# Block 0 goes into the FFN unscaled, and its inverse RMS is applied to the gate in PSUM and to the output rows

## The chip, the cores and the metric

The kernel runs on one core of one Trainium2 chip. A time is the device time of one execution in microseconds (us). Before the change the median of 9 runs is 244.38 us (243.91 to 245.1).

## What is computed

Two stages follow each other. The first is attention with four sink tokens and a causal window of 128, for 4 sequences of 768 tokens and 8 heads of 64. The second takes the heads side by side as x (3072 tokens of 512) through a normalisation and a gated FFN:

```
keep   = is_sink | in_window
a      = softmax(where(keep, q @ k.T / 8, -1e9));  attn = a @ v
x      = attn, heads side by side                       # 3072 x 512
xn     = x / sqrt(mean(x*x) + 1e-6) * rms_g
g, val = xn @ w_gate, xn @ w_val                        # 512 x 1536 each
out    = (g * sigmoid(g) * val) @ w_out                 # 1536 x 512
```

## The kernel before

The 3072 tokens are 24 blocks of 128 (six to a sequence), and four blocks are a group G of 512 columns for the FFN. Group 0 is worked on while its blocks are still being made: the list HAND cuts its FFN into 12 pieces f.0 to f.11, of which f.0, f.1, f.2, f.4, f.6 and f.7 take the first 256 columns (blocks 0 and 1), and f.0 is cut once more into block 0 and block 1 (`split`). Later groups are worked through whole, with the attention of coming blocks put between the parts.

A block g goes through these atoms, each named by a token of the string ORDER ("v.2.0/1" is atom 1 of v for block 2, half 0): t or T transpose q and k on TensorE (lines 281, 298); b puts the additive masks into PSUM by a matmul (382); s or S are the scores and their exp on ScalarE (394, 442); sk, sv, ss and a are the sinks (324 to 380, 489); v is the product with v, with reciprocal and normalisation on VectorE (504); q squares x with an accumulated sum (538); y makes the inverse RMS by six tiny VectorE instructions (557); xr scales the rows by it (610); x transposes the scaled rows and copies them to xnt, for blocks 0 and 1 with rms_g as a column gt (634, 647). Then mms (662) multiplies xnt by the weights: gate into `pg`, value into `pvl`, tanh on ScalarE, and `first` and `second` on VectorE make hT = (tanh(pg/2) + 1) * pg * pvl (lines 680 to 701). out_atoms (750) multiplies by w_out, and line 764 moves the result out of PSUM times 0.5. gt and gb (251, 263) bring rms_g to columns and to a full tile by float32 matmuls of one row.

Order is by hand: until group 1 the scheduler is off for all five engines, and each engine takes its instructions in the order in which the tokens of ORDER (849) issue them. w.N is a filler: a matmul of zeros, 512 columns wide, that nobody reads (242). ON_ACT and ON_DVE (220) say which of ScalarE and VectorE does a movable copy or square. PSUM has 8 banks of 512 float32 columns from one pool, and a tile waits until the bank's last reader is done. Loads are issued by GpSimd (POOL) in the order of the string at line 200: q, k, v of a block, g and u the six chunks of w_gate and w_val, o the halves of w_out. LOADS and the loops of group and run (887, 839) place what comes later.

## Time and profile before

| what | value |
|---|---|
| median of 9 runs | 244.38 us |
| the profiled execution, own time | 244.68 us |
| its span | 242.8 us |
| TensorE (PE) busy | 237.7 us (98%) |
| VectorE (DVE) busy | 164.0 us (68%) |
| ScalarE (ACT) busy | 133.7 us (55%) |
| GpSimd (POOL) busy | 107.3 us (44%) |
| first FFN matmul starts (line 668) | 15.26 us |
| granted TensorE clock, mean of the span | 0.993 |

The profile is one execution, and times are counted from the start of its span. Part 1 of its page gives the busy time of each engine, part 2 the span in 40 slices of 6.1 us: a digit is a busy share in tenths, and PEclk is the granted TensorE clock in tenths of full speed. A row of a timeline reads: start, duration (of several merged instructions from the first start to the last end), engine, line of the kernel, operation, output and input, shape, count, and in brackets the idle time before it with what ended it. A busy TensorE can still be slow: the duration of a matmul includes its way through the pipe, and at half clock it just lasts longer. The pitch, from one start to the next, is what TensorE really spends.

### The profile page before, as it was taken

What the parts mean: (1) busy time and instruction counts of PE and PEld (TensorE: products, weight loads), DVE (VectorE), ACT (ScalarE), POOL (GpSimd) and SP (SyncE); (2) the same over time, 40 slices, a digit from 0 to 9 for tenths busy, and PEclk for the clock granted to TensorE, in tenths of its full rate; (3) what the DMA queues carried; (4) which work ended last, traced back from release to release, by engine and by line L of the source; (5) the groups of instructions that cost most, each with busy time, mean ns of one, the idle gap of its engine ahead of it and who ended that gap; (6) DMA issues with size and microseconds to landing.
All of it is one profiled execution on the core that took longest, in us unless ns stands there. A gap on an engine that the chain in (4) does not pass through costs nothing.

```text
span 242.8 us, 5281 instructions
## 1 busy us (share of the span) xinstructions
PE 237.7 (98%) x2011; PEld 137.5 (57%) x2011; DVE 164.0 (68%) x390; ACT 133.7 (55%) x309; POOL 107.3 (44%) x145
## 2 busy tenths in 40 slices
PE   8999999999999999999999999999999999999995
PEld 3668888855877874444444444444444444444443
DVE  5767796894988798067879086869077884287800
ACT  3675648458788874666562567664565342333212
POOL 8977686589649870389992003034032000000000
PEclk9979999999999999999999999999999999999999
DMA  9999999999999995489999664002600003600022
GB/s 128 143 178 186 182 166 199 176 155 175 208 152 122 62 110 67 89 223 155 139 145 96 173 159 84 0 1 38 189 35 3 0 0 70 173 19 1 0 79 97
DMA packets 109291, 26.56 MB, mean 109 GB/s; under 512 B 98385, under 2 KB 106321, under 8 KB 109266
## 3 DMA queue, kind: packets, MB, share of 16 engines
q0 software_dynamic: 80704, 13.90, 77.2%
q1 hardware_dynamic: 27378, 12.00, 23.9%
q10 hardware_dynamic: 1184, 0.33, 0.6%
q8 instruction: 16, 0.26, 0.5%
q14 instruction: 9, 0.07, 0.1%
HBM read 28.31 MB, written 6.29 MB: 143 GB/s over the span
## 4 chain that ended last, share of the span: by engine, by line
PE 95%; DVE 1%; DMA 1%; SPq 1%; ACT 0%; issue 0%; ACTq 0%
PE pg L668 26%; PE pvl L668 26%; PE po L757 22%; PE pT L455 4%; PE pv L516 3%; PE pv L520 3%; PE pqk L237 2%; PE pT L386 2%; PE pw L245 1%; PE po L739 1%; DMA qkT<-qs 1%; SPq L629 1%; PE pxt L642 1%; PE pv L497 1%; PE pT L401 1%; PE pss L367 1%
## 5 line engine op out<-in xcount | busy, mean ns | idle before, releaser
L668 PE MATMUL pvl<-xnt,wv 128*128 128x512 bf16 (+2 forms) x440 | 74.6, 306 | 0.0
L668 PE MATMUL pg<-xnt,wg 128*128 128x512 bf16 (+2 forms) x440 | 73.8, 305 | 0.5 <-DVE xnt L654 0.3
L687 DVE SCALAR_TENSOR_TENSOR p<-th,pg 128x512 bf16<-128x512 bf16 x72 | 49.3, 684 | 26.1 <-ACT th L682 25.6
L682 ACT ACTIVATE th<-pg 128x512 bf16<-128x512 f32 x72 | 43.2, 602 | 38.3 <-PE pg L668 38.1
L757 PE MATMUL po<-wo,hT 128*128 128x512 bf16 x276 | 62.3, 379 | 0.0
L697 DVE TENSOR_TENSOR hT<-p,pvl 128x512 bf16<-128x512 bf16 x72 | 49.2, 686 | 6.2 <-PE pg L668 0.5
L668 PEld LDWEIGHTS <-wv 128*128 128x128 bf16 x440 | 38.3, 98 | 24.8 <-issue 0.2
L668 PEld LDWEIGHTS <-wg 128*128 128x128 bf16 x440 | 37.5, 98 | 23.3 <-issue 1.3
L431 POOL TENSOR_SCALAR_AFFINE_SELECT et<-et 128x512 bf16<-128x512 bf16 x30 | 20.6, 692 | 65.4 <-ACT et L465 62.2
L757 PEld LDWEIGHTS <-hT 128*128 128x128 bf16 x276 | 26.3, 98 | 29.5
L465 ACT ACTIVATE et<-pT 128x512 bf16<-128x512 f32 x72 | 38.1, 606 | 5.7 <-PE pT L455 5.5
L764 ACT ACTIVATE osb<-po 128x512 f32<-128x512 f32 x23 | 13.7, 596 | 34.1 <-PE po L757 34.1
L551 ACT ACTIVATE sq<-x 128x256 bf16<-128x256 bf16 x42 | 17.6, 423 | 13.5 <-DVE x L532 13.3
L121 POOL DMA_DIRECT2D v<-in_v_dram x24 | 21.7, 903 | 7.6 <-DMA wo<-in_moe_w_out_dram 5.1
L527 DVE RECIPROCAL rden<-pv 128x4 f32<-128x4 f32 x48 | 7.6, 173 | 23.1 <-PE pv L520 23.1
L108 POOL DMA_DIRECT2D qs<-in_q_dram x23 | 20.8, 906 | 2.7 <-issue 0.8
L108 POOL DMA_DIRECT2D ks<-in_k_dram x23 | 20.7, 899 | 1.6 <-DMA wg<-in_moe_w_gate_dram 0.5
L532 DVE TENSOR_TENSOR x<-pv,rden 128x256 bf16<-128x256 f32 x48 | 19.4, 421 | 0.8
L622 DVE SCALAR_TENSOR_TENSOR xr<-x,y,gb 128x512 bf16<-128x512 bf16 x22 | 16.9, 816 | 0.2
L436 POOL TENSOR_SCALAR_AFFINE_SELECT et<-et 128x512 bf16<-128x512 bf16 x24 | 15.9, 660 | 0.0
L520 PE MATMUL pv<-v,et 128*128 128x65 bf16 x160 | 12.4, 194 | 0.0
L455 PE MATMUL pT<-qkT 64*128 64x256 bf16 (+1 forms) x160 | 11.3, 261 | 0.0
(82 smaller groups left out, 184.3 us busy)
## 6 DMA issues: line engine op xcount, KB each, us to landing
out_dram<-osb SPq DMA_DIRECT2D x21, 256.0 KB, 2.4
v<-in_v_dram POOLq DMA_DIRECT2D x24, 128.0 KB, 7.6
qs<-in_q_dram POOLq DMA_DIRECT2D x23, 128.0 KB, 7.1
ks<-in_k_dram POOLq DMA_DIRECT2D x23, 128.0 KB, 7.0
wv<-in_moe_w_val_dram POOLq DMA_DIRECT2D x6, 256.0 KB, 8.9
wg<-in_moe_w_gate_dram POOLq DMA_DIRECT2D x6, 256.0 KB, 8.6
wo<-in_moe_w_out_dram POOLq DMA_DIRECT2D x2, 768.0 KB, 11.1
out_dram<-osb SPq DMA_DIRECT2D x4, 128.0 KB, 3.1
```

Source lines behind the costliest of these rows:

```text
L108: nc.gpsimd.dma_start(out=tl, in_=src[b, :, t * P:(t + 1) * P, :].rearrange("h t d -> t h d"),)
L121: nc.gpsimd.dma_start(out=V16[b][:, t, :, 0:D], in_=v[b, :, t * P:(t + 1) * P, :].rearrange("h t d -> t h d"),)
L431: nc.gpsimd.affine_select(out=ev[:, :, 0, :], in_=ev[:, :, 0, :], compare_op=ALU.is_ge, fill=0.0, base=0, pattern=[[0, x], [1, P]], channe ...
L455: nc.tensor.matmul(out=banks[u][hi][:, j * w:(j + 1) * w], lhsT=QKT[b][pr, 1, hp, t * P:(t + 1) * P], rhs=QKT[b][pr, 0, hp, t * P:t * P + ...
L465: nc.scalar.activation(out=ets[u][:, hi].rearrange("p j n c -> p (j n c)"), in_=banks[u][hi], func=ACT.Exp, scale=inv_sqrt_d,)
L520: nc.tensor.matmul(out=dest, lhsT=E[(g, h, 0)], rhs=V16[b][:, t, h, :], start=(t == 0), stop=True, skip_group_check=True,)
L532: nc.vector.tensor_tensor(out=X16[g][:, heads_of(g, u), :], in0=view()[:, :, 0:D], in1=RDEN.pop((g, u)).unsqueeze(2).to_broadcast((P, 4, D ...
L668: nc.tensor.matmul(out=ps[:, i * w + c0:i * w + c0 + n], lhsT=w_sb[:, kt, ft * P:(ft + 1) * P], rhs=XNT[G][:, kt, cols], start=(kt == 0), ...
L682: LAST_TANH[0] = nc.scalar.activation(out=st["th"], in_=st["pg"], func=ACT.Tanh, scale=0.5).ins
L687: nc.vector.scalar_tensor_tensor(out=st["p1"], in0=st["th"], scalar=1.0, in1=st["pg"], op0=ALU.add, op1=ALU.mult,)
L697: LAST[0] = nc.vector.tensor_tensor(out=HT[key][:, i:i + n, cols], in0=st["p1"].rearrange("p (n c) -> p n c", n=n), in1=st["pvl"].rearrang ...
L757: nc.tensor.matmul(out=st["po"], lhsT=HT[(G, ft // 4)][:, ft % 4, tb * P:(tb + 1) * P], rhs=wo[:, ft, :], start=(ft == 0), stop=(ft == FTN ...
```

## The change

Block 0 is transposed as it comes from attention (X16), without xr. Its inverse RMS y is turned into a row that is equal in all partitions: a float32 matmul with y broadcast to 128 columns as the weights and a float32 identity as the moving operand, copied from PSUM to `yb`. In the six pieces of group 0 with blocks 0 and 1 in their columns, a new atom `scaled` multiplies block 0's 128 columns of each gate part in PSUM by yb, before the tanh. The value part stays unscaled; the missing factor comes in with block 0's output rows, which are moved out of PSUM times half0 = y / 2 in place of 0.5.

The string ORDER is another one as a whole, and ON_ACT, ON_DVE and the order of the loads are others too. It has 12 fillers in place of 9. gt and gb stand together, ahead of block 2's transposes.

```diff
+    half0 = const.tile([P, 1], FP32, name="half0")
-    raw = [opool.tile([P, DM], FP32, name="osb") for _ in range(3)]
+    raw = [opool.tile([P, DM], FP32, name="osb") for _ in range(4)]
+    ident32, yb = raw[3][:, 0:P], raw[3][:, P:2 * P]
...
+        nc.vector.tensor_copy(out=ident32, in_=ident)
...
-        for x in ("v0 q2 v1 k2 u0 g0 u2 v2 g1 g2 k3 u1 q3 g5 g3 u3 v3 g4 u4 v5 q4 u5 "
-                  "k4 q5 q6 k5 k6 o0 v4 o1 k7 q7 k8 v6 q9 v8 q8 v7 k9 v9").split():
+        for x in ("v0 v1 q2 u0 k2 v2 g0 g2 u2 g1 u1 k3 q3 g3 g4 u3 v3 g5 q4 u5 q5 u4 "
+                  "v5 k4 k6 v9 k5 k9 q6 v4 o0 o1 q7 k7 v7 v6 k8 v8 q9 q8").split():
...
+            if g0 == 0:
+                nc.vector.tensor_scalar(
+                    out=half0, in0=Y[0], scalar1=0.5, scalar2=None, op0=ALU.mult,
+                )
...
+    def a_yb():
+        ps = []
+
+        def mm():
+            ps.append(bank("pyb"))
+            nc.tensor.matmul(
+                out=ps[0][:, 0:P], lhsT=Y.pop(0).to_broadcast((P, P)), rhs=ident32,
+                start=True, stop=True,
+            )
+        return [mm, lambda: mover("yb", "a")(out=yb, in_=ps[0][:, 0:P])]
...
-            xr = XR.pop(g)
+            xr = XR.pop(g) if g else X16[g].rearrange("p h d -> p (h d)")
...
+        def scaled():
+            pg = st["pg"].rearrange("p (n c) -> p n c", n=n)[:, :, 0:P]
+            nc.vector.tensor_tensor(
+                out=pg, in0=pg, in1=yb.unsqueeze(1).to_broadcast((P, n, P)), op=ALU.mult)
+
         if split:
             return [lambda: half(0, 0), lambda: half(0, 1), lambda: half(1, 0), tanh,
-                    lambda: half(1, 1), first, second]
+                    lambda: half(1, 1), first, second, scaled]
+        if G == 0 and cols.start == 0:
+            return [gate, tanh, val, first, second, scaled]
...
-            nc.scalar.mul(osb, st["po"], 0.5)
+            nc.scalar.mul(osb, st["po"], half0 if G == 0 and tb == 0 else 0.5)
```

The part of ORDER from block 0's product with v to the second gate half of f.0, before:

```
        v.0.1/2 s.1.0/1 q.0.1/0 sk.0/0 s.1.0/2 s.0.1/2 v.0.0/2 q.0.0/0 y.0/0 gb/0 v.1.0/0
        v.1.0/1 b.2.0/0 sv.0/0 sv.0/1 y.0/1 y.0/2 v.1.0/2 y.0/3 y.0/4 w.74/0 gt/0 v.1.1/0
        t.2.0/0 y.0/5 xr.0/0 v.1.1/1 v.1.1/2 t.2.1/0 x.0/0 b.1.1/0 gt/1 q.1.0/0 t.2.0/1 s.1.1/0
        x.0/1 f.0/1 w.73/0 sv.0/2 q.1.1/0 y.1/0 y.1/1 y.1/2 y.1/3 y.1/4 y.1/5 sk.0/1 ss.0.2.1/0
        f.0/0 t.2.1/1 xr.1/0 x.1/0 s.2.0/0 gb/1 s.1.1/2 s.1.1/1 sv.0/3 ss.0.2.1/1 a.2/0 s.2.0/1
        s.2.0/2 x.1/1 f.0/2 f.0/3 v.2.0/0 v.2.0/1 v.2.1/0 f.0/4 f.1/0 v.2.0/2 v.2.1/1 q.2.0/0
```

and after:

```
        v.0.1/2 w.88/0 s.1.0/2 q.0.0/0 v.1.0/0 b.1.1/0 gt/0 gb/0 t.2.0/0 v.1.0/1 q.0.1/0 y.0/0
        y.0/1 y.0/2 v.1.0/2 s.0.1/2 x.0/0 y.0/3 gt/1 t.2.0/1 q.1.0/0 y.0/4 y.0/5 v.1.1/0 v.1.1/1
        v.1.1/2 yb/0 w.91/0 w.80/0 sv.0/0 t.2.1/0 s.1.1/0 x.0/1 q.1.1/0 y.1/0 y.1/1 y.1/2 sk.0/1
        y.1/3 y.1/4 yb/1 y.1/5 b.2.0/0 f.0/1 sv.0/2 ss.0.2.1/0 xr.1/0 f.0/0 x.1/0 sv.0/1 t.2.1/1
        s.2.0/0 f.0/7 s.1.1/1 s.1.1/2 ss.0.2.1/1 sv.0/3 s.2.0/1 w.90/0 s.2.0/2 x.1/1 a.2/0 f.0/2
        v.2.0/0 v.2.1/0 v.2.0/1 v.2.0/2 v.2.1/1 v.2.1/2 q.2.0/0 q.2.1/0 y.2/0 y.2/1 y.2/2 y.2/3
```

## The prediction, as it was put on record

> **What bounds the kernel now.** I read the engine table and the 40 slices first, then TensorE's timeline of the first 30 us beside VectorE's, then the busy times and granted clock in stretches, then the waits. Page, parts 1 and 2:

> ```profile
> PE 237.7 (98%) x2011; PEld 137.5 (57%) x2011; DVE 164.0 (68%) x390; ACT 133.7 (55%) x309; POOL 107.3 (44%) x145
> PEclk9979999999999999999999999999999999999999
> ```

> TensorE is busy 98% of the span. From about 27 us its matmuls follow each other at their own pitch, and the list of waits has only one later one that counts, 0.5 us for the transposes by DMA near 102 us, behind the same row of SyncE's queue in both kernels. So a change in block 0 pays only through what TensorE does before some 30 us. There the clock has a hole. Stretches of the first 22 us (width, then PE, PEld, DVE, ACT, POOL busy with instructions, PEclk, DMA share, GB/s):

> ```profile
> 5.20:8.61 3.41, 3.24 (x47) 1.89 (x46) 2.08 (x5) 1.40 (x4) 3.41 (x5) 1.00 2.17 139
> 8.61:12.02 3.41, 3.41 (x33) 2.11 (x33) 2.79 (x15) 2.69 (x8) 3.41 (x6) 1.00 1.57 142
> 12.02:15.44 3.42, 3.42 (x33) 2.39 (x33) 2.12 (x9) 2.41 (x9) 3.21 (x5) 0.50 1.50 165
> 15.44:18.85 3.41, 3.06 (x54) 2.46 (x53) 1.86 (x5) 2.73 (x7) 1.94 (x4) 1.00 1.66 190
> ```

> For 3.41 us TensorE ran at half speed, after a stretch in which it was "busy" throughout, but largely with float32 matmuls of one row (gb 1.05 us, gt 0.98 us, rows below). TensorE's timeline around it (start, us, engine, line, op):

> ```profile
> 8.87 1.12 PE L268 MATMUL pgb<-osb,gb 1*128 1x512 f32 x2
> ...
> 11.04 1.05 PE L257 MATMUL pgt<-gb,osb 1*128 1x1 f32 x8
> ...
> 13.29 0.63 PE L642 MATMUL pxt<-ident,xr 128*128 128x128 bf16 x4
> ...
> 15.26 0.69 PE L668 MATMUL pvl<-xnt,wv 128*128 128x128 bf16 x8
> ...
> 18.02 0.61 PE L668 MATMUL pg<-xnt,wg 128*128 128x128 bf16 x8 [0.33 <-DVE xnt L654]
> ```

> And VectorE's, for what these wait on:

> ```profile
> 11.84 0.39 DVE L618 TENSOR_SCALAR xr<-x,y 128x512 bf16<-128x512 bf16 x1
> ...
> 17.27 0.69 DVE L654 TENSOR_TENSOR xnt<-pxt,gt 128x512 bf16<-128x512 bf16 x1 [0.60 <-PE pxt L642]
> ...
> 24.67 0.68 DVE L687 SCALAR_TENSOR_TENSOR p<-th,pg 128x512 bf16<-128x512 bf16 x1
> 25.26 1.28 DVE L697 TENSOR_TENSOR hT<-p,pvl 128x512 bf16<-128x512 bf16 x2
> 26.82 0.69 DVE L687 SCALAR_TENSOR_TENSOR p<-th,pg 128x512 bf16<-128x512 bf16 x1 [0.28 <-ACT th L682]
> ```

> The reader should see that block 0's scaled rows are ready at 11.84 + 0.39 = 12.23 us, and TensorE comes to transpose them only at 13.29. The inverse RMS is not what TensorE waits for. Its real wait is block 1's copy (17.27 to 17.96), which holds the second half of the first gate until 18.02.

> **The change, part by part.** *Removed:* block 0's scaling (0.39 us of VectorE) and its place ahead of the transposes. On TensorE this is worth 0; with the clock full it would have come to the transposes some 0.5 us earlier, still after 12.2. Below zero nothing, above zero at most those few tenths.

> *Added on TensorE:* the broadcast matmul (float32, 128 columns) and fillers, 12 for 9, all three extra ones in mid-stream (five against two). The broadcast has no row. From below: one gt matmul of one column, 0.98 / 4 = 0.245 us. From above: gb with 512 columns, 1.05. By columns between them: 0.45. A filler of 512 columns is 0.22 us at full and 0.43 at half clock (the seven at the start begin 0.43 apart), so three are 0.65 to 1.3 us. Where TensorE waits anyway they are free.

> *Added on VectorE:* six scalings of 128x256 float32 in PSUM. No row reads and writes PSUM in place. Nearest is x<-pv,rden, 128x256 from PSUM, 0.42 us; a 512-wide copy of 0.68 bounds it above, 0.17 (the reciprocal's floor) below. I take 0.42, 2.5 us in all, four of them before 28 us. The copy of the broadcast row, half0 and the float32 identity are small (0.2, 0.1, 0.2 by the same floor). Against this, gb's copy (0.68) goes to ScalarE and xr of block 0 (0.39) goes. Each scaling stands between a gate and its tanh, so it also keeps a PSUM bank longer. The output's scale by half0 instead of 0.5 costs nothing: the same ACTIVATE of 0.60.

> *Moved:* v1, u0 ahead of k2, v2 ahead of the first gate weights. Loads land in the order of issue, 0.8 to 1.0 us per q, k or v and 1.2 to 2.1 per weight chunk, so by the bytes ahead of it g0 lands near 15.2 us (14.56 before) and u1 near 20.9 (21.6 before); both are in time in the walk below. Later, block 11's load changes places with block 14's in POOL's queue and now stands behind block 7's masks (63.2 to 65.8 us before). With 7.1 us to landing and 4.7 for its transposes by SyncE, which now pass one store, it is there near 77.5; block 10's scores, the first to read it, come at 81.6, so this costs nothing. gb and gt now stand together, ahead of block 2's transposes and block 1's second attention product.

> **The sum, by TensorE's queue.** I walk the new order with the pitches of the old timeline (start to start: 0.216 for 512 columns, 0.056 for 128, 0.03 for the 65-wide products; two rows of scores run side by side, so 16 matmuls take what 8 do) and hold each step until what it waits for is done. Both kernels are alike to 8.87 us. Then: filler to 9.09; block 1's product waits for the fourth exp (four end at 7.31 + 2.15 = 9.46) and takes to 9.75; masks 0.43, gt 0.98 to 11.2; gb 1.05. In the stretch 8.61 to 12.02 that is 0.2 + 0.2 + 0.25 + 0.43 us of bfloat16 work, 1.1, where the kernel before had some 1.25 and was slowed all the same. So I expect the half clock again from 12.02 to 15.44. Then gb ends at 12.5; eight transposes (0.107 each, as the four at 13.29) 13.35; the product's eight 13.8; broadcast about 0.65 14.45; two fillers 0.85 15.3; sink selection 15.5. From there at full clock t 0.22, scores 0.45, masks 0.43, first value half 0.45, sinks 0.28, first gate half 0.45: 17.78. VectorE then scales this half (17.9 to 18.3) *before* block 1's copy, which is queued behind it, 0.69: 19.0, against 18.02. The second gate half is queued behind that copy and all of TensorE behind it: **+1.0 us**. From there TensorE is full in both, and the lateness stays to the end. The profiled execution took 244.68 us (span 242.8); with 1.0 it is 245.7. The median of the nine runs is 0.3 below the profiled one, so I forecast **245.4**.

> [...]

> **Rivals.** *The fillers hold the clock (faster).* If it stays full from 12.02, the same queue gives gb to 12.25, transposes 12.7, product 12.95, broadcast 13.4, fillers 13.83, first value half 15.05, first gate half to 16.3; block 1's copy ends 17.65 and the second half starts at 17.7, 0.3 before. Before, block 2's products also stood still from 18.52 to 18.74 for an exp; here the exps are done first (18.05), and the value half behind the products ends at 19.1 and not at 19.75, 0.65 ahead. If that is kept: 244.38 - 0.65 = 243.7. For it: five fillers between 8.9 and 22 us. Against: less bfloat16 work ahead of 12.02 than before. It decides once PEclk is 1.00 there.

> *Full clock, but VectorE gives it back (level).* Between 22 and 28 us VectorE has 0.28 us idle before (third row above); three scalings come in. Each `first` or `second` takes 0.60 from start to start (24.67 to 25.26), and the matmuls of f.2 to f.4 wait for banks that these steps free. Walked on with that, the gate of f.4 starts at 27.55 (27.56 before) and that of f.8 at 36.9 (36.84): 244.4 to 244.7.

> *VectorE becomes the bound (slower still).* Half clock and the scalings at 0.68: four times 0.26 more on a queue without slack, 246.4.

> *It does not do what it says:* that the first FFN matmul, at 15.26 before, does not come earlier is my forecast itself (about 16.6).

> **How the numbers follow.** Forecast 0.52 (slower 0.50, same 0.02); clock held 0.20 (faster); given back 0.18 (same 0.14, faster 0.02, slower 0.02); VectorE bound 0.10 (slower). So faster 0.22, same 0.16, slower 0.62, where 0.2% (0.49 us) is about what a measurement of this kernel can tell from no change. The range reaches from the held clock (243.7) to nearly the VectorE case: 246.2.

> **What would show it.** PEclk 0.50 again for a stretch near 12 to 15 us; first L668-type value matmul near 16.6 us, second gate half near 19.0, waiting for block 1's copy; TensorE without gaps after 30 us. I am wrong if PEclk stays 1.00 up to 20 us, if the first value matmul comes before 15.3 us, or if TensorE waits for VectorE's hT or p after 23 us by more than a few tenths.

## The result, and the profile after

The changed kernel takes 246.35 us (median of 11 runs, 244.98 to 247.07) against 244.40 (34 runs beside them, 243.41 to 245.26): **1.0078 times as long, interval [1.0063, 1.0093]**, slower by 1.95 us. I had forecast 245.4 in a range of 243.7 to 246.2. The direction was right; the size was a half too small, and the time lies 0.15 above the range.

The profiled execution of the changed kernel (246.70 us, span 245.0) is an odd one, as its own page says. Parts 1 and 2:

```profile
PE 237.6 (97%) x2016; PEld 136.7 (56%) x2016; DVE 166.1 (68%) x402; ACT 131.2 (54%) x305; POOL 107.1 (44%) x145
PEclk9999999999999999999999999999999999999999
```

Here the clock never fell, and yet it is one of the slower executions. Its list of TensorE's waits says why (engine, line, waited for: us in total, times, longest):

```profile
PE pvl L688 <- DMA wv<-in_moe_w_val_dram: 1.1, 1, 1.1
PE pg L688 <- DMA wg<-in_moe_w_gate_dram: 0.7, 1, 0.7
```

and TensorE's timeline shows where:

```profile
15.14 0.61 PE L688 MATMUL pvl<-xnt,wv 128*128 128x128 bf16 x8
...
16.78 0.62 PE L688 MATMUL pg<-xnt,wg 128*128 128x128 bf16 x8 [0.71 <-DMA wg<-in_moe_w_gate_dram]
...
18.58 0.61 PE L688 MATMUL pg<-xnt,wg 128*128 128x128 bf16 x8
...
23.00 1.05 PE L688 MATMUL pvl<-xnt,wv 128*128 128x256 bf16 x8 [1.06 <-DMA wv<-in_moe_w_val_dram]
```

The first value half comes 0.12 before that of the old kernel (15.26, at half clock), then TensorE stands for weights twice, and the second gate half, at 18.02 before, starts at 18.58.

Every run lists the mean granted clock of its span. A span without a drop has 0.998 to 1.00; before's profiled one, with 3.41 us at half clock (12.02 to 15.44), has 0.993, and 0.992 or 0.993 counts here as one such stretch. Sorted by that, medians in us, with the number of executions in brackets (the kernel before is taken from the runs beside e1 to e12; with those beside e13 to e18 it is 26 of 106 that have such a stretch):

| kernel | full clock | one half-clock stretch | more |
|---|---|---|---|
| before (88 runs) | 244.10 (64) | 244.73 (17) | 7 |
| after (12) | 245.04 (3) | 246.62 (9) | 0 |

This table is the result in brief. The change costs 0.94 us at full clock, 1.89 when both have one half-clock stretch, **and** it turns an execution with a stretch from the exception (24 of 88) into the rule (9 of 12). The profile of before that I worked from (clock 0.993) is of this rarer kind.

### The profile page after: what moved, and what is told of

Same layout as the page of the kernel before. It is cut to its first block, busy times and chain, and to the rows that moved or that the text cites. A ratio compares the mean times of both kernels' runs of the same rounds, so it can differ in the third digit from the quotient of the medians.

```text
span 245.0 us, 5298 instructions
## 1 busy us (share of the span) xinstructions
PE 237.6 (97%) x2016; PEld 136.7 (56%) x2016; DVE 166.1 (68%) x402; ACT 131.2 (54%) x305; POOL 107.1 (44%) x145
## 4 chain that ended last, share of the span: by engine, by line
PE 84%; DMA 5%; POOL 4%; DVE 2%; ACT 2%; SPq 1%; issue 1%; POOLq 0%; ACTq 0%
PE pvl L688 24%; PE pg L688 24%; PE po L784 22%; DMA wv<-in_moe_w_val_dram 4%; PE pT L458 4%; PE pv L519 2%; PE pv L523 2%; PE pqk L240 1%; PE po L766 1%; POOL v L121 1%; DMA qkT<-qs 1%; SPq L647 1%; POOL wg L141 1%; DVE p L707 1%; DVE hT L717 1%
## 5 line engine op out<-in xcount | busy, mean ns | idle before, releaser
L791 ACT ACTIVATE osb<-po 128x512 f32<-128x512 f32 x22 | 13.1, 595 | 33.2 <-PE po L784 33.2
L554 ACT ACTIVATE sq<-x 128x256 bf16<-128x256 bf16 x42 | 17.6, 423 | 14.6 <-DVE x L535 14.5
L108 POOL DMA_DIRECT2D qs<-in_q_dram x23 | 20.9, 908 | 9.0 <-DMA wo<-in_moe_w_out_dram 6.0
L121 POOL DMA_DIRECT2D v<-in_v_dram x24 | 21.6, 902 | 2.0 <-DMA wv<-in_moe_w_val_dram 1.4
L523 PE MATMUL pv<-v,et 128*128 128x65 bf16 x160 | 12.2, 194 | 0.0
L413 ACT ACTIVATE etp<-pT 128x512 bf16<-128x512 f32 x16 | 8.6, 598 | 6.0 <-PE pT L404 6.0
```

Of the source, the lines that this page charges most:

```text
L108: nc.gpsimd.dma_start(out=tl, in_=src[b, :, t * P:(t + 1) * P, :].rearrange("h t d -> t h d"),)
L121: nc.gpsimd.dma_start(out=V16[b][:, t, :, 0:D], in_=v[b, :, t * P:(t + 1) * P, :].rearrange("h t d -> t h d"),)
L523: nc.tensor.matmul(out=dest, lhsT=E[(g, h, 0)], rhs=V16[b][:, t, h, :], start=(t == 0), stop=True, skip_group_check=True,)
L554: nc.scalar.activation(out=sq, in_=xh, func=ACT.Square, scale=MS_SCALE, accum_out=MS[g - i][:, i, u:u + 1],)
```

## The experiments

**Which part of the change costs it?** In the first four expectations theory A puts the loss on the written order (where the fillers and the late weights are parts that can be tried by themselves), theory B on the new arithmetic and its extra links in VectorE's chain. e1 has the new order, engines and loads with the old arithmetic; e2 the new arithmetic in the old order.

```diff
 e1: after, without yb, half0 and the scalings
-yb/0 yb/1 f.0/7 f.1/5 f.2/5 f.4/5 f.6/5 f.7/5
+y.0/5 xr.0/0 x.0/0
 e2: before, with yb, half0 and the scalings
+b.1.1/0 yb/0 ... f.0/1 yb/1 ... f.0/7 f.0/3 ... f.k/5 f.k/1
-xr.0/0
```

> The new order, loads and engine choices with the old arithmetic: block 0's rows are scaled before their transposes, no broadcast row, no scaling in PSUM, output times 0.5. Theory A (the written order costs the time: half clock after the float32 cluster gt, gb, mid-stream fillers, and gate and value weights that land too late): about +1.2 to +1.8 us over the kernel before, so nearly the whole loss stays. Theory B (the unscaled block costs it: broadcast, six scalings, longer chains): within 0.4 us of the kernel before.

Measured 245.72, ratio 1.0065 [1.0043, 1.0087]; 245.0 at full clock (6 of 12), 246.61 with a stretch (6). At either clock this is the changed kernel to 0.05: **the written order with its loads carries the loss; in that order the arithmetic costs nothing that shows.**

> The old order and loads with the new arithmetic: broadcast matmul behind block 1's second mask, scalings of the gate in PSUM ahead of each tanh, half0 at the output. Theory A: +0.2 to +0.5 us (0.30 us of broadcast on TensorE, measured in the changed kernel, and some tenths of VectorE). Theory B: +1.2 us or more, with TensorE waiting for VectorE between 20 and 30 us.

Measured 247.06, ratio 1.0104 [1.0066, 1.0141]; 246.94 at full clock (4 of 6), 2.8 more than before. So theory A's forecast for e2 fell and theory B's came: in an order not made for it the new arithmetic is dear. Its list of waits has

```profile
PE pxt L663 <- DVE xr L641: 0.9, 1, 0.9
```

and VectorE's timeline ahead of that wait (start, us, ..., in brackets the idle time)

```profile
35.07 0.42 DVE L740 TENSOR_TENSOR pg<-pg,osb 128x256 f32<-128x256 f32 x1
36.22 0.69 DVE L708 SCALAR_TENSOR_TENSOR p<-th,pg 128x512 bf16<-128x512 bf16 x1 [0.72 <-ACT th L703]
36.83 0.75 DVE L641 SCALAR_TENSOR_TENSOR xr<-x,y,gb 128x512 bf16<-128x512 bf16 x1
37.49 0.43 DVE L740 TENSOR_TENSOR pg<-pg,osb 128x256 f32<-128x256 f32 x1
```

The scaling itself is small (0.42). What hurts is the round it puts into the chain: `p` waits 0.72 us for a tanh that had to wait for the scaling at 35.07, and block 3's xr, queued behind `p`, holds TensorE's transposes. That is 0.9 of the 2.8; more of it lies in other waits of 0.2 to 0.3 us each for VectorE and ScalarE.

**Fillers and loads.** e3 leaves out five fillers in mid-stream (w.88 w.91 w.80 w.90 w.89); e4 has the old order of loads.

> The changed kernel without its five fillers in mid-stream. If they only cost TensorE time: 0.6 to 1.1 us faster than the changed kernel (0.22 each at full clock, 0.43 at half), less where they stand in waits. If they hold the clock up: as slow as the changed kernel or slower, with the half clock in every execution. If they stand in waits altogether: no change.

Measured 246.59, ratio 1.0079 [1.0051, 1.0108]; half clock in 8 of 12, twice for two stretches. No time comes back: other waits take the fillers' places.

> The changed kernel with the loads in the order of the kernel before. If the late weights cost (waits of 0.7 us for the first gate chunk and 1.1 us for the second value chunk in the changed kernel's profile): 0.7 to 1.7 us faster than the changed kernel, about 1.000 to 1.004 of the kernel before, and no wait for wg or wv in the profile. If the loss is the clock's and the fillers': within 0.3 us of the changed kernel.

Measured 247.07, ratio 1.0109 [1.0069, 1.0149], half clock in 6 of 6. In its profile block 1's product waits 0.8 us just ahead of the float32 matmuls, and no weights are late. The profile puts this wait down to an exp, but the exps start at 7.86 as in e18 (below), where the product goes on at 10.06; here it goes on at 10.54, when v1, which the old order of loads brings later, has landed at 10.50 (9.56 in e18). The old loads don't fit the new order, and late weights aren't what a usual execution loses.

**What makes the clock fall?** From here the letters mean something else: theory A blames the one-row float32 matmuls gt and gb, theory C something else. e5 and e6 bring rms_g by DMA instead, e7 puts gb beside gt in the old kernel, e8 puts gb apart from gt in the new one, in place of the filler w.88.

```diff
 e5 (before) and e6 (after), with gt and gb out of ORDER
+    nc.sync.dma_start(
+        out=gb, in_=moe_rms_g.rearrange("(o d) -> o d", o=1).to_broadcast((P, DM)),
+    )
+    nc.sync.dma_start(out=gt, in_=moe_rms_g.rearrange("(kt p) -> p kt", p=P))
 e7
-q.0.0/0 y.0/0 gb/0 v.1.0/0 ... w.74/0 gt/0 v.1.1/0
+q.0.0/0 y.0/0 v.1.0/0 ... w.74/0 gt/0 gb/0 v.1.1/0
 e8
-v.0.1/2 w.88/0 s.1.0/2 ... gt/0 gb/0 t.2.0/0
+v.0.1/2 gb/0 s.1.0/2 ... gt/0 t.2.0/0
```

> The kernel before, with rms_g brought into columns and into the full tile by two DMAs of SyncE in place of the float32 matmuls gt and gb (tokens gt and gb out of ORDER). Theory A (the one-row float32 matmuls are what brings the half clock): granted clock 1.00 in every execution, where the kernel before has it in 17 of 24; time 243.0 to 244.0, at most the 2.0 us that the two matmuls take earlier. Theory C (the clock is decided by something else, such as how long TensorE stands between its first transposes and 12 us): executions at 0.993 stay, or grow more, since the float32 matmuls also filled time; 244.2 or more.

> The changed kernel with the same edit. Theory A: clock 1.00 in every execution (3 of 12 with the matmuls) and 244.0 to 245.0, which is the changed kernel's 245.0 at full clock less what the two matmuls stood on the path. Theory C: executions at 0.993 stay, 246 or more.

> The kernel before with its token gb/0 moved behind gt/0, so that the float32 matmuls stand together as in the changed kernel, nothing else. Theory A (together they bring the half clock more often): 0.993 in more than half of the executions, against 7 of 24, median 244.8 or more. Theory C: share as before, 244.0 to 244.5.

> The changed kernel with gb/0 in the place of the filler w.88, where TensorE waits for an exp anyway, and so apart from gt, nothing else. Theory A: 0.993 in fewer than half of the executions against 9 of 12, and gb partly stands in the wait: 244.7 to 245.3. Theory C: share as in the changed kernel; 245.8 to 246.3.

| run | median, ratio | full clock | with half-clock stretches |
|---|---|---|---|
| e5 | 244.95, 1.0038 [1.0021, 1.0055] | 244.88 (8) | 4 of 12 |
| e6 | 246.32, 1.0100 [1.0064, 1.0137] | 246.03 (4) | 2 of 6 |
| e7 | 244.69, 1.0023 [1.0000, 1.0046] | 244.49 (7) | 5 of 12 |
| e8 | 245.26, 1.0039 [1.0022, 1.0055] | 245.09 (10) | 2 of 12 |

Theory A falls in its strict form: the clock halves without any float32 matmul of one row (e5, e6). In e8 the share of half clock fell as theory A had it, and e7 went the same way (5 of 12, against 6 of 29 beside it), but not to the more than half that theory A asked for. The DMAs that take their place aren't free either: the loads behind them land about 1.1 us later (q of block 1 at 7.43 in e5, 6.27 in the profile of before), so neither is faster. But where the float32 matmuls stand counts: e8 takes 1.1 us off the median by one token moved into a filler's place, with the full-clock time unchanged. So I formed a **window theory** from the profiles. In before's the granted clock changes at 5.20, 12.02 and 15.44 us and next at 244.13, behind the end of the span: steps of 2, 1 and 67 times 3.413 us. In e8's it is 0.50 from 11.89 to 15.30, in e18's (below) full from 6.82 and 0.50 from 13.64 to 17.06. A window is a stretch of 3.41 us, counted from the first full clock, which comes at another time in each execution (5.20 and 6.82 here). The theory, a guess from these profiles, is that a window with too little bfloat16 streaming is followed by one at half clock.

**Is the rest of it weights (theory L) or VectorE's queue (theory V)?** e9, e10 and e11 start from e8, e12 from before. In e9 and e12 the pieces f.0 to f.3 multiply by the first chunk of w_val in place of their own weights (the result is not the layer's).

```diff
 e9, e12
-                    lhsT=w_sb[:, kt, ft * P:(ft + 1) * P],
+                    lhsT=wv[:, kt, (ft % 2) * P:(ft % 2 + 1) * P],   (pieces f.0 to f.3)
 e10
-k2 v2 g0 g2
+k2 g0 v2 g2
 e11
-s.2.0/0 f.0/7 s.1.1/1 ... x.1/1 a.2/0 f.0/2
+s.2.0/0 s.1.1/1 ... x.1/1 f.0/7 a.2/0 f.0/2
```

> The changed kernel with gb ahead of block 1's product (as in e8), and the pieces f.0 to f.3 multiply by the first chunk of w_val, for gate and value alike, in place of their own weights: same matmuls, no wait for the chunks g0 to g2, u1, u2; the result is not the layer's. Theory L (at full clock the new order waits for weights that land late): 244.0 to 244.3 at full clock, against e8's median of 245.1 at full clock. Theory V (VectorE's queue, with the scalings in it, gives the pace): 244.9 to 245.3.

> The kernel before with the same replacement of weights, nothing else; the result is not the layer's. Theory L: its order comes to the weights after they land, so nothing to win: 243.8 to 244.2 at full clock (244.0). Theory V says nothing on it. If it gains as much as e9, the weights are a price of both and not of the change.

> e8 with the load of g0 ahead of v2 (v2 g0 becomes g0 v2), nothing else. Theory L: the first gate half no longer waits for g0, 0.3 to 0.7 us off where nothing later gives it back, 244.4 to 244.8 at full clock; if the later wait for u1 takes it back, 245.1. Theory V: 245.1.

> e8 with f.0's scaling (f.0/7) issued behind block 1's copy (x.1/1) in place of ahead of it, nothing else. My prediction put 0.4 of its 1.0 us on this place: then the second gate half starts 0.4 earlier and the time at full clock is 244.6 to 244.8. Theory L: the lead is lost at u1, 245.0 to 245.2.

Full-clock medians: e9 244.91 (8 of 12), e12 244.11 (9), e10 244.77 (9), e11 244.60 (9); ratios of all runs 1.0031 [1.0003, 1.0058], 0.9993 [0.9960, 1.0026], 1.0029 [1.0004, 1.0054] and 1.0029 [1.0004, 1.0055]. Theory L falls for the usual execution: with all weights there, only 0.2 comes back. (e10 alone would speak for it: 244.77 is inside theory L's 244.4 to 244.8.) The kernel before, run beside each of them, is alike at full clock (244.08 beside e8, 244.12 beside e9 to e12, 244.23 beside e13 to e15), so e8 to e15 can be set against each other. e11 comes lowest, 0.5 under e8 and near the 0.4 that I had put on the scaling's place, but not for that reason. e11's VectorE and TensorE:

```profile
16.71 0.69 DVE L674 TENSOR_TENSOR xnt<-pxt,gt 128x512 bf16<-128x512 bf16 x1 [0.65 <-PE pxt L662]
17.32 0.42 DVE L739 TENSOR_TENSOR pg<-pg,osb 128x256 f32<-128x256 f32 x1
```

```profile
17.79 0.61 PE L688 MATMUL pg<-xnt,wg 128*128 128x128 bf16 x8
```

The copy is done at 17.40, but the second gate half goes into the tile of PSUM that is being scaled, and starts at 17.79, after the scaling (17.32 + 0.42). It waits for both, whatever their order; in e10, with the scaling first, it starts at 17.61. So the 0.5 has no place in the profile. Medians of some nine executions that spread over 0.7 to 1.3 us are, by my estimate, not good for less than about 0.3.

**Two last questions.** e13 tests the window theory on the old kernel with one more filler; e14 puts e8, e10 and e11 together, and e15 takes three fillers out of e14.

```diff
 e13 (before)
-w.74/0 gt/0
+w.74/0 w.75/0 gt/0
 e15 (e14)
-w.80/0 w.90/0 w.89/0
```

> The kernel before with one more filler (w.75) beside w.74, ahead of gt, nothing else. Window theory (the clock is set per window of 3.41 us, whose place against the program's start differs from execution to execution, and it halves after a window with less than some 1.2 us of bfloat16 streaming in it): before's thin windows are those that begin 8.4 to 9.1 us in, with 1.07 to 1.18; 0.22 more lifts all of them over 1.28. So half clock in at most 1 of 12 executions, against 24 of 88, and 243.9 to 244.3 at full clock, as the kernel before (244.1), since the filler stands in the slack before the second gate half. If the share stays at 3 or more of 12, the rule is not this one.

> The changed kernel with gb early (e8), f.0's scaling behind block 1's copy (e11) and g0 loaded ahead of v2 (e10). If the two add up, 244.2 to 244.4 at full clock (245.1 less 0.5 and 0.3); if what is left is TensorE's added work (the broadcast row 0.30 and two more fillers 0.43 of matmuls ahead of f.8), 244.5 to 244.7, no better than e11.

> e14 without the fillers w.80, w.90 and w.89 (0.65 us of matmuls). If TensorE's added work is what is left of the loss at full clock: 0.4 to 0.6 below e14, 243.9 to 244.3. If the fillers stand in waits, as e3 had it: as e14 within 0.15. Window theory: its thinnest window loses at most 0.2 us of streaming, so the share of half clock stays or rises, 3 to 6 of 12.

e13: half clock in 1 of 12, 244.33, ratio 0.9997 [0.9980, 1.0014]. This is as the window theory had it, but the kernel before beside it dropped only twice in 17, so it isn't proof; and it is no faster. e14: 245.55, ratio 1.0064 [1.0041, 1.0087], 245.07 at full clock (3 of 6); e15: 245.46, ratio 1.0052 [1.0033, 1.0071], 245.36 at full clock (5 of 6). The gains of e10 and e11 don't add up. The fillers aren't what is left either: e15 is no faster, and its list of waits has in their place

```profile
PE pg L688 <- DVE pg L739: 0.7, 1, 0.7
```

which is the second gate half waiting for the scaling. No version here beats the kernel before.

e16 is the kernel before, e17 and e18 the changed one, each run once more for a profile of the other kind.

> The kernel before, unchanged, for a profile of an execution whose clock stays full (the one on the page had the half clock). If the half clock is mostly hidden in this order: span 242.2 to 242.6, block 0's and 1's second gate half at 17.2 to 17.6 in place of 18.02, the chunk f.8 at 36.3 to 36.7 in place of 36.84.

> The changed kernel, unchanged, for a profile of an execution with the half clock (the one on the page had none, and two long waits for weights). With it: span 244.4 to 245.2, and by the window theory less than 1.2 us of bfloat16 streaming in the window ahead of the drop; no wait for weights above 0.5 us, since TensorE comes to them later. At full clock instead: a span of 243.3, and waits for weights under 0.8 us in all.

> As e17, once more, since 3 of 12 executions have no half clock and loads take longer in some executions than in others.

e16 came at full clock (244.59, span 242.9): its second gate half starts at 17.28 as expected, but a chunk of w_gate that lands late (0.7 us) puts f.8's gate at 37.02. e18 with one half-clock stretch (246.49, span 244.8), e17 with two in a row (247.98). Neither e17 nor e18 waits for weights by more than 0.2 us. e18 in stretches of its windows (width, busy time of PE, PEld, DVE, ACT, POOL with instructions, PEclk, DMA share, GB/s):

```profile
6.82:10.23 3.41, 2.86 (x51) 1.77 (x49) 2.14 (x9) 2.38 (x5) 3.41 (x5) 1.00 1.76 133
10.23:13.64 3.41, 3.41 (x36) 2.23 (x34) 2.03 (x12) 1.87 (x6) 3.41 (x7) 1.00 1.86 161
13.64:17.06 3.42, 3.42 (x24) 1.86 (x24) 2.74 (x12) 2.86 (x9) 2.52 (x5) 0.50 1.45 198
```

The window ahead of the drop is "busy" for all of its 3.41 us; the one before, with an idle half microsecond, brings no drop. What it lacks shows when the bfloat16 columns of the matmuls that start in a window are added up (2,400 columns counted as 1 us, rounded from the 512 that take 0.216 us from start to start; matmuls on 64 rows as a half, on 32 output columns as a quarter, which is my choice):

| windows | streaming, us |
|---|---|
| followed by half clock (before, e4, e8, e9, e17 twice, e18) | 1.13, 1.10, 1.02, 1.07, 1.07 and 1.12, 1.10 |
| half-clock windows not followed by another (before, e4, e8, e9, e17's second, e18) | 1.58, 1.34, 1.39, 1.39, 1.50, 1.50 |
| thinnest from 4 us on in the profiles without a drop | 1.28 or more in thirteen; 1.12 in e6's window 4.18 to 7.60 |

With one exception, early in e6, a line at about 1.2 us parts them. The line was drawn on these windows themselves. Of what was forecast by it, e17 and e18 held (1.07 and 1.10 ahead of the drop) and e13 fits; e15 did not, with 1 of 6 where 3 to 6 of 12 were expected. By this count the float32 matmuls matter because they fill a window without streaming much: gt and gb take 2.0 of the 3.41 us. With the two side by side, next to the wait for an exp, 25 of 38 executions have a drop (after, e1, e3, e17, e18), and 6 of 6 in e4; with gb apart (e8 to e11, e14 and e15) it is 16 of 60. That the place counts is shown by e8; that the clock goes by streamed columns is only what fits.

## Why the prediction was wrong, point by point

- *The inverse RMS is not what TensorE waits for, worth 0:* right. e1, which still waits for it, takes the same time at the same clock.
- *Half clock again:* right in 9 of 12 executions. The 1.1 us of bfloat16 work that I counted ahead of it is what e18 has (1.10); for the kernel before I had 1.25, where the columns give 1.13. I put the drop at 12.02 to 15.44; it moves with the execution (13.64 to 17.06 in e18, 11.92 to 18.75 in e17), as the first full clock does: 4.09 us after the start of the span in after's profile, 5.20 in before's, 6.82 in e18's. In before's and e18's the drop comes 6.82 us behind it. TensorE had hardly stood idle: of the 3.41 us ahead of the drop it was busy for 3.12 in e17 and for all 3.41 in before and e18.
- *The walk:* first value half 16.6 and second gate half at 19.0, behind scaling and copy. With the half clock, e18 has:

```profile
18.54 0.43 DVE L739 TENSOR_TENSOR pg<-pg,osb 128x256 f32<-128x256 f32 x1 [1.94 <-ACT vsk L357]
18.88 0.68 DVE L674 TENSOR_TENSOR xnt<-pxt,gt 128x512 bf16<-128x512 bf16 x1
```

```profile
16.89 0.69 PE L688 MATMUL pvl<-xnt,wv 128*128 128x128 bf16 x8
...
17.81 0.62 PE L688 MATMUL pg<-xnt,wg 128*128 128x128 bf16 x8
...
19.62 0.61 PE L688 MATMUL pg<-xnt,wg 128*128 128x128 bf16 x8
```

  The mechanism is as written: scaling, copy, then the second gate half. **The step that failed is the end of the sum: "From there TensorE is full in both, and the lateness stays to the end", by which "+1.0 us" was all.** Half clock against half clock (e18, span 244.8, and the profile of before, 242.8) the change costs 2.0. Up to the second gate half it is 1.60 (19.62 against 18.02) in place of 1.0. Block 1's product goes on at 10.06, where I had 9.46, and gt and gb stand behind it. But 0.55 of this 0.60 is not the new order: the exps start at 7.86 in e18 and at 7.31 in before, since TensorE reached full clock at 6.82 in the one execution and at 5.20 in the other. Block 0's first transposes show it, in e18 and then in before:

```profile
5.82 0.63 PE L240 MATMUL pqk<-ident,qs 128*128 128x128 bf16 x4
```

```profile
5.52 0.39 PE L237 MATMUL pqk<-ident,qs 128*128 128x128 bf16 x4
```

  In e16, the kernel before with full clock only from 6.46, the exps start at 7.75. So as far as the second gate half the walk was good to about 0.1 in this execution. Then the lateness grows: from there to f.8's gate e18 takes 19.45 and before 18.82, 0.63 more. These are f.8's gate in e18 and in before:

```profile
39.07 1.06 PE L688 MATMUL pg<-xnt,wg 128*128 128x128 bf16 x16
```

```profile
36.84 1.06 PE L668 MATMUL pg<-xnt,wg 128*128 128x128 bf16 x16
```

  TensorE is not full there. The filler w.89 is 0.22 (the only matmul more in that stretch; e3, without it, still takes 19.63), and the rest is small stops, the longest 0.26 ahead of block 2's transposes, which wait for VectorE's xr (23.59 + 0.75 = 24.34):

```profile
23.59 0.75 DVE L640 SCALAR_TENSOR_TENSOR xr<-x,y,gb 128x512 bf16<-128x512 bf16 x1
```

```profile
24.39 0.40 PE L662 MATMUL pxt<-ident,xr 128*128 128x128 bf16 x4
```

  0.2 comes back after f.8's gate.
- *Minus 0.3 to the median:* the second failure. The profiled execution and the median are of different kinds: the profile had the half clock, most executions of before have it not (244.10 against 244.73). The 1.0 was reckoned from one half-clock execution to another, so nothing was to be taken off: 244.68 + 1.0 = 245.7. With the 0.6 by which the lateness grows it is 246.3, and measured was 246.35.
- *Prices:* the broadcast matmuls 0.30 in after's profile, 13.09 to 13.39 (estimated 0.45), and a scaling 0.43 (0.42). Fillers: that they stand in waits was right (e3, e15). *Block 11's load costs nothing:* no sign against it; from f.8's gate to the end 206.2 us in after's profile, 206.0 before.
- *Loads, "both are in time in the walk below":* wrong in the profiled execution: g0 landed at 16.73 (I had 15.2) and u1 at 22.96 (20.9), and TensorE stood for each. In a usual one it costs some 0.2 (e9).
- *Rivals.* "Full clock, but VectorE gives it back" had f.8's gate at 36.9 and 244.4 to 244.7; at full clock after takes 245.04, and e10, e11 and e14, which differ from it in a few places, start that gate at 37.11, 37.16 and 36.84 (its own profile, behind two waits for weights, at 38.78). So the walk was good and the price 0.3 too low. "VectorE bound" (246.4) has the right time for a wrong reason: in e18 TensorE waits at most 0.3 us at a time for VectorE. My own mark for being wrong, "PEclk stays 1.00 up to 20 us", fits 3 executions of 12, and in the one of them that was profiled the first value matmul comes before 15.3 us, too (15.14).

What stays open: the 0.94 at full clock lies in the order (e1). A good part of it has a place: from the second gate half to f.8's gate TensorE takes 19.45 to 19.50 us in all six profiles of the new order in which no load stops it there (e4, e8, e9, e10, e17 and e18; e10 at full clock throughout), and 18.82 or 18.83 in the three of the old order (before, e5 and e7). But none of weights, g0's place, the scaling's place or fillers gives the loss back alone, and together they don't add up. Of the 1.89 with the half clock the walk's 1.0 and the 0.6 behind it have a place; the other 0.3 have none. Why the half clock costs 1.6 in the new order and 0.6 in the old was only compared, not tested: in the old kernel f.8's gate starts at 36.84 with the half clock (its first profile) and at 36.59 and 37.02 without (e13, e16), so there most of it took the place of waits.

## What to carry to other kernels

Ask of every run which clock its execution was granted, and set like against like before a difference is explained; a profile can be of the rarer kind. Where TensorE does little streaming for some microseconds (here one-row float32 matmuls that take 2.0 of 3.41 us, a wait, small products), try to spread it out: one token moved into a filler's place took 1.1 us off the changed kernel's median (e8, with half clock in 2 of 12 executions against 9 of 12). An operation that is cheap by its own duration costs what its place in the queues costs: the same broadcast and six scalings cost nothing that shows in one order and 2.8 us in another.
